# Reordering the join of a spectral block and the hand-over to its feed-forward: the order of early products, bank choices, load order and one LayerNorm tile on Trainium2

## The chip, the cores and the metric

The kernel runs on one core of one Trainium2 chip. The metric is the device time of one execution in microseconds (us); lower is better. Before the change the median of 4 runs is 252.41 us (251.09 to 253.37). The engines are named as the profile names them: PE (TensorE matmuls), PEld (its weight loads), DVE (VectorE), ACT (ScalarE), POOL (GpSimd) and SP (SyncE, which only issues transfers here). PSUM, the memory that matmuls write, has 8 banks.

## What is computed

```python
h = _layernorm(x) * (1 + ca) + sa
x = x + ga * irfft2(rfft2(h) * (w_r + 1j * w_i))
h = _layernorm(x) * (1 + cb) + sb
x = x + gb * ((silu(h @ w_gate) * (h @ w_up)) @ w_down)
```

`x` is 2048 x 640 in bf16. The six vectors sa, ca, ga, sb, cb, gb are the six parts of `silu(c) @ w_mod`, where `w_mod` is 640 x 3840. The spectral filter is 2048 x 321 complex; `w_gate` and `w_up` are 640 x 1728 and `w_down` is 1728 x 640.

## The kernel before, in words

**Stages.** The kernel has four stages. First, the forward transform along the 640 columns and its first step along the 2048 rows, tile by tile (16 tiles of 128 rows). Second, what this text calls the join: for the 81 frequency slots l (a slot holds four related columns), the last step of the forward row transform, the product with the filter, and the first steps back. Third, the rest of the inverse transform for the 16 row tiles t (line 1138), together with the residual and the statistics of the second LayerNorm. Fourth, the feed-forward over five chunks of 2, 4, 4, 4 and 2 tiles. The first of these chunks multiplies plainly (`gu_plain`, `down_plain`); the others use a scheme with fewer products (`gate_up_pairs`, `down_pair`).

**The join's groups.** The slots are in 21 groups (lines 509 to 511, `NG` = 21): groups 0 to 3 are l = 48 to 63, group 4 is l = 0 and 80, groups 5 to 16 are l = 1 to 47, groups 17 to 20 are l = 64 to 79. A group has four slots, except group 4 (two) and group 5 (three). For each group:

- `stage_a` (line 561): one matmul per slot (line 567) into the buffer `xps` of two banks, banks 2 and 3 for even groups and 4 and 5 for odd ones. Then DVE makes two products with the filter (`prod`, line 588): half 0 with the table `Wn`, half 1 with the table `Wv`, the filter stored in reversed order. So the matmuls of group g+2 write the banks that the products of group g read.
- `stage_b` (line 590): two matmuls per slot (line 595) add the parts, into bank g % 2; ACT copies the result to SBUF (line 598).
- `stage_c` (line 608) and `evac` (line 619): one more matmul per slot (line 616), and the copy to SBUF, mostly of two groups at once, out of banks 6 and 7. Afterwards POOL makes a turned copy (`rot`, line 644).

`wsum` (line 402) makes the third row of `Wn` or `Wv`, the sum of the other two, for a range of slots; products of these slots wait for it. `Wv` is read back from DRAM by two DMAs of line 426, the second one called `wflip_r` in the profile.

**Where the data of a group comes from.** `t2_pe` (line 533) transposes the slots of groups 0 to 4 on PE, ACT or DVE evacuates them. `t2_dma` (line 515) does so for the others by DMA transposes issued by SP: number 0 for l = 1 to 15, 1 for 16 to 31, 2 for 32 to 47, 3 for 64 to 79. For each of them POOL adds one column (`sa_add`, line 553, instruction at line 559) before `stage_a` may read it.

**Order.** Everything is issued in an order written out by hand, and every engine and the SP queue executes its own instructions in this order. Lines 673 to 685 begin the join: modulation matmuls `ga_mod` (line 649), the four `t2_pe`, `stage_a` of groups 0 and 1. The loop at line 686 then does, for each g: `sa_add(g + 4)`, `wsum` on POOL, `stage_a(g + 2)`, `stage_b(g)`, `stage_c` of earlier groups.

**Modulation of the second LayerNorm.** sb and cb come from 50 small matmuls (line 571) with `wm_r[:, :, 1:3]`, put inside `stage_a` of the last six groups, after its first matmul. `wm_r` is loaded by SP: part 0 early, parts 1 and 2 together at line 526 (1600 KB), part 3 at line 528.

**The hand-over.** In the loop over t at line 1138 the DVE instruction of line 1152 adds the residual and sums the row. For tiles 0 and 1, the first feed-forward chunk, `ln2_sq` (ACT, line 748) sums squares at t = 1 and 2, `ln2_var` (DVE, lines 752 to 754) and `ln2_pow` (POOL, line 758) come at t = 3, `ln2_xn` (DVE, line 762) at t = 4 and 5, and `ln2_tr` (line 776) at t = 5 issues the DMA transpose on SP. `ln2_mod` (POOL line 784 for four of the five blocks, ACT line 790 for the fifth) applies 1 + cb and sb. The first matmuls that need it are those of `gu13` (line 972), put at t = 15 just ahead of the last tile's matmuls. `load_gu` (line 731) loads a range of gate and up columns: 0 to 512 and 512 to 1024 ahead of the loop, 1024 to 1664 right after the DMA transpose.

**The first chunk.** The loop at line 1186 goes over 13 column blocks of 128, in the order 0, 6, 1, 7, 2, 8 and so on, with 10 matmuls a block (line 984).

Of the kernel before, what the change touches and what calls it, by code (L numbers as in the profile page):

```python
# [18 lines left out]
NT, P = 16, 128  # L19
NL = 81  # L20
NW = 256
NC5 = 5
# [133 lines left out]
def adaln_block_kernel(ctx, tc, A_x, A_w_r, A_w_i, B_x, B_w_gate, B_w_up, B_w_down, c, w_mod, out):  # L156
    nc = tc.nc
# [57 lines left out]
    Wn = rW.cut(0, [3, NT, NW])  # L215
    Wv = rW.cut(24576, [3, NT, NW])
# [108 lines left out]
    if True:  # L325
# [140 lines left out]
        for t in range(2, NT + 2):  # L466
# [4 lines left out]
            u = t + 2  # L471
# [39 lines left out]
    NG = len(groups)  # L511
    if True:
# [10 lines left out]
        t2_dma(0)  # L523
        t2_dma(1)
        t2_dma(2)
        nc.sync.dma_start(wm_r[:, :, 1:3, :], wm_m[:, :, 1:3, :])
        t2_dma(3)
        nc.sync.dma_start(wm_r[:, :, 3, :], wm_m[:, :, 3, :])
        nc.sync.dma_start(Htab[:], H_dram)
        nc.sync.dma_start(RI[:], RI_dram)  # L530
# [30 lines left out]
        def stage_a(g):  # L561
            ls = groups[g]
            n = len(ls)
            xps = banks(2 + 2 * (g % 2), 2, [4, 256])
            for i, l in enumerate(ls):
                B2, j = B2of[l][0:2]
                nc.tensor.matmul(xps[:, i, 0:192], lhsT=B2[:, j, :], rhs=KS2, start=True, stop=True)  # L567
                if i == 0:
                    for c5 in {NG - 6: (0, 1), NG - 5: (0, 1), NG - 4: (2, 3), NG - 3: (2,), NG - 2: (4,), NG - 1: (3, 4)}.get(g, ()):
                        for k in range(NC5):  # L570
                            nc.tensor.matmul(psum[:, 2 + 2 * (g % 2), 192 + c5:193 + c5],
                                             lhsT=wm_r[:, k, 1 + g % 2, 128 * c5:128 * c5 + 128],
                                             rhs=sc_col[:, k:k + 1], start=(k == 0), stop=(k == NC5 - 1))
            PP = rM.cut(1536 * (g % 4), [3, 2, NT, 2, n])
            prod(g, PP, xps, 0)
            prod(g, PP, xps, 1)
            return PP

# [10 lines left out]

        def stage_b(g, PP):  # L590
            n = len(groups[g])
            yps = banks(g % 2, 1, [4, 128])
            for ps in (1, 0):
                for i in range(n):
                    nc.tensor.matmul(yps[:, i, :], lhsT=_rev(PP, 64 * n * ps + i, [[n, 128]]), rhs=identb[:],  # L595
                                     start=(ps == 1 and i == 0), stop=(ps == 0 and i == n - 1))
# [11 lines left out]
        def stage_c(u):  # L608
            for g in units[u]:
                ls = groups[g]  # L610
                n, l0 = len(ls), ls[0]
                eps_ = banks({NG - 4: 4, NG - 3: 5, NG - 2: 1, NG - 1: 0}.get(g, 6 + (l0 // 4) % 2), 1, [4, 128])
                Y2 = Y2s.pop(g)
                for i, l in enumerate(ls):
                    kv = {0: 1, 80: 2}.get(l, 0)
                    nc.tensor.matmul(eps_[:, i + 4 - n if l0 else i, :], lhsT=Y2[:, i, :], rhs=Ktab[:, 128 * kv:128 * kv + 128],  # L616
                                     start=True, stop=True)

        def evac(u):
            g, l0 = units[u][0], groups[units[u][0]][0]  # L620
            if l0 == 0:
                edge = rY.cut(4096, [2, 128])
                nc.scalar.copy(edge[:], banks(6, 1, [4, 128])[:, 0:2, :])
                for i in range(2):
                    nc.gpsimd.tensor_copy(Em[:, :, :, 64 * i].rearrange("p v q -> p q v"),
                                          edge[:, i, :].rearrange("p (q v) -> p q v", v=2))
            elif g == NG - 2:
                nc.vector.tensor_copy(ep_views(l0, 4), banks(1, 1, [4, 128]).rearrange("p i q -> p q i"))
            elif g == NG - 1:
                nc.scalar.copy(ep_views(l0, 4), banks(0, 1, [4, 128]).rearrange("p i q -> p q i"))  # L630
            else:
                n = len(groups[g]) + 4
                (nc.vector.tensor_copy if g == NG - 6 else nc.scalar.copy)(
                    ep_views(l0, n), banks(4 if g == NG - 4 else 6, 2, [8, 128])[:, 8 - n:8, :].rearrange("p i q -> p q i"))
                if g < NG - 4:
                    rots.extend((l0, n, i) for i in range(1 if g == NG - 6 else 2))
# [36 lines left out]
        PPs, Y2s, rots = {}, {}, []  # L673
        ga_mod(320, 5, range(3))
        t2_pe(0)
        wsum(Wv, 48, 64, nc.vector)
        t2_pe(1)
        ga_mod(320, 5, range(3, NC5))
        PPs[0] = stage_a(0)
        t2_pe(2)  # L680
        t2_pe(3)
        wsum(Wn, 80, 81, nc.gpsimd)
        wsum(Wv, 80, 81, nc.gpsimd)
        PPs[1] = stage_a(1)
        ga_mod(0, 6, range(2))
        for g in range(NG + 1):
            sa_add(g + 4 if g > 0 else 0)
            for W, lo, hi in {0: ((Wv, 0, 16),), 1: ((Wv, 16, 32),), 3: ((Wv, 32, 48),), 11: ((Wn, 64, 80),), 13: ((Wv, 64, 80),)}.get(g, ()):
                wsum(W, lo, hi, nc.gpsimd)
            if g + 2 < NG:  # L690
                PPs[g + 2] = stage_a(g + 2)
            if g == 0:
                ga_mod(0, 6, range(2, NC5))
            if g == NG - 3:
                nc.vector.tensor_copy(modcols[:, 2, :], psum[:, 2, 192:197])
                nc.vector.tensor_copy(modcols[:, 3, :], psum[:, 4, 192:197])
                nc.vector.tensor_scalar_add(one_p_cb[:], modcols[:, 3, :], 1.0)
            if rots:
                l0, n, i = rots.pop(0)
                rot(l0, n, slice(0, 64), nc.gpsimd, (i,))  # L700
            if g < NG:
                Y2s[g] = stage_b(g, PPs.pop(g))
            for u, gs in enumerate(units):
                if gs[-1] + (1 if gs[0] >= NG - 2 else 3 if gs[0] == 4 else 2) == g:
                    stage_c(u)
                    evac(u)
            if g == NG - 1:
                rot(40, 8, slice(0, 64), nc.vector, (1,))
                nc.vector.tensor_tensor(RI[:, 1], RI[:, 1], ga_bc[:], ALU.mult)
# [18 lines left out]
    nc.sync.dma_start(Wp13[:, :, 0:64], B_w_gate[:, 1664:1728].rearrange("(c5 dp) f -> dp c5 f", dp=P))  # L728
    nc.sync.dma_start(Wp13[:, :, 64:128], B_w_up[:, 1664:1728].rearrange("(c5 dp) f -> dp c5 f", dp=P))

    def load_gu(lo, hi):
        nc.sync.dma_start(Wgu[:, 0, :, lo:hi], B_w_gate[:, lo:hi].rearrange("(c5 dp) f -> dp c5 f", dp=P))
        nc.sync.dma_start(Wgu[:, 1, :, lo:hi], B_w_up[:, lo:hi].rearrange("(c5 dp) f -> dp c5 f", dp=P))

    load_gu(0, 512)
    load_gu(512, 1024)

    x1 = rM.cut(0, [NT, D], F32)
    st2 = const.tile([P, NT, 2], F32, name="st2")
# [395 lines left out]
    if True:  # L1135
        VTs = {0: s1er(0), 1: s1er(1)}
        nc.vector.tensor_copy(gb_bc[:, 0:320], mod_bc(3, 0, 7))
        for t in range(NT):
            if t and t + 1 < NT:
                s1em(t + 1)  # L1140
                VTs[t + 1] = s1er(t + 1)
            VT = VTs.pop(t)
            if t == NT - 1:
                fin13 = gu13(0, at_of(0))
            ops = banks(6 * (t % 2), 2, [4, 256])[:, :, 0:160]
            for h in range(2):
                nc.tensor.matmul(ops[:, 2 * h:2 * h + 2], lhsT=VT[:, 4, :], rhs=RI[:, 1, 2 * h:2 * h + 2, :],
                                 start=True, stop=False)
                for rr in range(2):
                    nc.tensor.matmul(ops[:, 2 * h + rr], lhsT=VT[:, 2 * h + rr, :], rhs=RI[:, 0, 2 * h + rr, :],  # L1150
                                     start=False, stop=(rr == 1))
            nc.vector.scalar_tensor_tensor(x1[:, t, :].rearrange("p (m r) -> p m r", r=4), ops.rearrange("p r m -> p m r"), 1.0,
                                           x_sb[:, t, :].rearrange("p (m r) -> p m r", r=4), ALU.mult, ALU.add,
                                           accum_out=st2[:, t, 0:1])
            if t in (8, 11):
                gu_dma(GS[0][:], B_w_gate, t // 11 * 2, 2, t == 8)
            if 1 <= t <= 2:
                ln2_sq(t - 1)
            if t == 3:
                ln2_var(0, 2)  # L1160
                ln2_pow(0, 2)
            if 4 <= t <= 5:
                ln2_xn(0, t - 4)
            if t == 5:
                ln2_tr(0)
                load_gu(1024, 1664)
            if t in (5,7,9,11):
                ln2_sq(2 + (5,7,9,11).index(t))
            if t in (10, 13):
                ln2_mod(0, range(4) if t == 10 else range(4, 5))  # L1170
# [9 lines left out]
    for ci, (t0, n) in enumerate(chunks):  # L1180
# [3 lines left out]
            gate_up_pairs(ci, ATc, [lambda i=i: (ln2_xn_act(2, i), wd_tables(i, 1)) for i in range(4)] + [lambda: wd_tables(3, 0)] if ci == 1 else [])  # L1184
        else:
            for fc in range(NFC - 1):
                ff = fc if fc == 12 else fc // 2 + 6 * (fc % 2)
                half = gu_plain(ci, ATc, ff, (c3f, c22f)[fc % 2])
                half(0)
                half(1)  # L1190
# [91 lines left out]
```

## Time and profile before

| what | value |
|---|---|
| median of 4 runs | 252.41 us (251.09 to 253.37) |
| the profiled execution, its own time | 253.37 us |
| its span, first to last instruction | 251.6 us |
| granted TensorE clock in the span | 1.000 |
| PE busy | 243.5 us, 97% of the span |
| DVE, ACT, POOL busy | 210.5, 163.0, 74.9 us |
| moved by DMA | 34.43 MB, mean 137 GB/s |
| join and its end (first DVE product to first matmul of tile 0) | 40.4 to 66.4 us |
| inverse transform by tile | 66.4 to 84.7 us |
| first feed-forward chunk | 84.7 to 106.7 us |
| the other four chunks | 106.7 us to the end |

All times on a line of the profile count from the first instruction. A line of the timeline or of the chain gives start, length, engine, source line and how many instructions follow each other (x8); what stands in square brackets is how long the engine was idle before and what ended that. Matmuls are pipelined: the length of one overlaps the next, so the pace is read from the starts.

### The profile page before, as it was taken

The page shows a single profiled execution, that of the slowest core. Times are in us where ns is not written, and L with a number is a line of the kernel's source. Part 1 is how long each engine was busy: PE and PEld are TensorE (multiplying, and loading weights), DVE is VectorE, ACT ScalarE, POOL GpSimd, SP SyncE. Part 2 cuts the span into 40 slices and gives each one's busy share as a digit, 9 for nine tenths or more (in the row PEclk, how much of TensorE's full clock was granted, in tenths as well). Part 3 has the DMA queues.
Part 4 walks back from the last instruction along what each step waited for, and adds up shares of the span by engine and source line. Part 5 has one row for each costly group of instructions (what it writes and reads, how often), then busy time and mean ns, then how long its engine had stood idle before and what let it go on. Part 6 is the DMA issues. An engine that isn't in the chain of part 4 may idle for free.

```text
span 251.6 us, 6472 instructions
## 1 busy us (share of the span) xinstructions
PE 243.5 (97%) x2512; PEld 200.5 (80%) x2512; DVE 210.5 (84%) x524; ACT 163.0 (65%) x300; POOL 74.9 (30%) x122
## 2 busy tenths in 40 slices
PE   8999996999999999999999999999999999999994
PEld 3778875999789788788877778886768887779973
DVE  4798886998889998679997898879995978895895
ACT  3778664988788688678963577774267676235740
POOL 8487756695020905000001910000340000440000
PEclk9999999999999999999999999999999999999999
DMA  7999989999999999700005021001411000211001
GB/s 222 391 352 328 314 353 172 237 277 399 273 339 300 251 274 161 150 26 0 3 0 107 0 65 43 3 3 33 77 49 52 3 0 3 52 53 56 3 0 52
DMA packets 45760, 34.43 MB, mean 137 GB/s; under 512 B 21731, under 2 KB 42658, under 8 KB 45346
## 3 DMA queue, kind: packets, MB, share of 16 engines
q1 hardware_dynamic: 43936, 30.00, 42.8%
q0 software_dynamic: 1504, 3.95, 6.9%
q8 instruction: 19, 0.31, 0.5%
q10 hardware_dynamic: 290, 0.08, 0.1%
q14 instruction: 11, 0.09, 0.1%
HBM read 26.72 MB, written 4.72 MB: 125 GB/s over the span
## 4 chain that ended last, share of the span: by engine, by line
PE 72%; SPq 9%; DMA 9%; issue 4%; DVE 2%; POOL 1%; ACT 1%; DVEq 0%; POOLq 0%; ACTq 0%
PE psum L1014 32%; PE psum L897 19%; PE psum L984 9%; DMA rW<-wflip_r 4%; PE psum L595 3%; PE psum L877 3%; DMA rW<-rL 3%; SPq L277 2%; PE psum L567 2%; SPq L273 2%; DMA rM<-in_w_mod_dram 2%; SPq L275 2%; PE psum L972 2%; PE psum L616 2%; SPq L279 1%
## 5 line engine op out<-in xcount | busy, mean ns | idle before, releaser
L1014 PEld LDWEIGHTS <-rW 128*128 128x128 bf16 (+1 forms) x528 | 46.9, 98 | 5.7 <-issue 0.2
L1014 PE MATMUL psum<-rW 128*128 128x256 bf16 (+1 forms) x240 | 27.1, 259 | 0.0
L911 POOL TENSOR_TENSOR rM<-rM,rL 128x320 f32<-128x320 f32 x6 | 5.9, 977 | 68.3 <-ACT rL L910 68.3
L897 PEld LDWEIGHTS <-rE 128*128 128x128 f16 (+1 forms) x196 | 19.1, 97 | 7.7
L1014 PE MATMUL psum<-rY,rW 128*128 128x256 bf16 (+1 forms) x96 | 24.0, 259 | 0.0
L984 PE MATMUL psum<-rW 128*128 128x256 bf16 (+1 forms) x170 | 23.1, 291 | 0.0
L897 PE MATMUL psum<-rE 128*128 128x320 f16 (+1 forms) x147 | 22.3, 299 | 0.0
L588 DVE TENSOR_TENSOR rM<-psum,rW 128x384 bf16<-128x384 f32 (+2 forms) x42 | 20.0, 543 | 1.5 <-PE psum L567 0.9
L984 PEld LDWEIGHTS <-rW 128*128 128x128 bf16 x170 | 16.6, 98 | 3.8
L1014 PEld LDWEIGHTS <-rE 128*128 128x128 f16 x192 | 17.4, 98 | 2.4
L897 PEld LDWEIGHTS <-rX 128*128 128x128 bf16 (+1 forms) x151 | 14.5, 97 | 5.4
L758 POOL TENSOR_TENSOR rstd<-rstd,mhalf 128x4 f32<-128x4 f32 (+2 forms) x4 | 4.8, 1190 | 46.4 <-DVE rstd L754 46.4
L1050 DVE TENSOR_TENSOR rH<-psum,rW 128x512 bf16<-128x512 f32 x21 | 14.5, 690 | 4.7 <-PE psum L1014 2.8
L1046 ACT COPY rH<-psum 128x512 f32<-128x512 f32 x21 | 12.3, 586 | 8.7 <-PE psum L1014 7.0
L1053 ACT COPY rX<-psum 128x512 f32<-128x512 f32 x21 | 12.3, 587 | 6.9 <-PE psum L1014 6.9
L1040 ACT COPY rW<-psum 128x512 f32<-128x512 f32 x21 | 12.3, 586 | 6.8 <-PE psum L1014 6.6
L1068 DVE TENSOR_TENSOR rX<-rH,rL 128x512 bf16<-128x512 bf16 x21 | 8.9, 424 | 9.1 <-ACT rL L1066 9.0
L382 DVE SCALAR_TENSOR_TENSOR rE<-rE,mv,psum 128x648 bf16<-128x648 f32 (+1 forms) x17 | 14.2, 844 | 2.1 <-PE psum L318 1.5
L1054 DVE TENSOR_TENSOR rX<-psum,rX 128x512 f32<-128x512 f32 x21 | 14.4, 686 | 1.7 <-ACT rX L1053 1.6
L897 PE MATMUL psum<-rA,rX 128*128 128x320 bf16 (+1 forms) x98 | 15.6, 299 | 0.0
L1014 PE MATMUL psum<-rH,rW 128*128 128x256 f16 (+1 forms) x96 | 15.1, 259 | 0.1
L1014 PE MATMUL psum<-rE,rY 128*128 128x256 f16 (+1 forms) x96 | 15.1, 259 | 0.0
(198 smaller groups left out, 678.0 us busy)
## 6 DMA issues: line engine op xcount, KB each, us to landing
out_dram<-rA SPq DMA_DIRECT2D x31, 80.0 KB, 1.6
rM<-in_w_mod_dram SPq DMA_DIRECT2D x3, 800.0 KB, 9.2
rX<-in_A_x_dram SPq DMA_DIRECT2D x3, 640.0 KB, 7.4
rA<-in_B_w_down_dram SPq DMA_DIRECT2D x2, 960.0 KB, 11.1
rM<-in_w_mod_dram SPq DMA_DIRECT2D x1, 1600.0 KB, 8.2
rY<-in_B_w_gate_dram POOLq DMA_DIRECT2D x2, 768.0 KB, 7.2
rW<-in_B_w_gate_dram SPq DMA_DIRECT2D x2, 640.0 KB, 8.0
rW<-in_B_w_up_dram SPq DMA_DIRECT2D x2, 640.0 KB, 8.2
```

The lines of the kernel that those rows point to most:

```text
L382: nc.vector.scalar_tensor_tensor(Zv[:, h], Cv[:, h], mv[:, t, 0:1], zps[:, h], ALU.mult, ALU.subtract)
L588: nc.vector.tensor_tensor(PP[:, :, hl], xv[:, :, hl], in1, ALU.mult)
L595: nc.tensor.matmul(yps[:, i, :], lhsT=_rev(PP, 64 * n * ps + i, [[n, 128]]), rhs=identb[:], start=(ps == 1 and i == 0), stop=(ps == 0 and ...
L897: nc.tensor.matmul(o, lhsT=lhsT, rhs=rhs, start=start, stop=stop, skip_group_check=True)
L984: nc.tensor.matmul(gu[u], lhsT=Wgu[:, u, c5, ff * 128:(ff + 1) * 128], rhs=h2T[:, :, c5, :], start=(c5 == 0), stop=(c5 == NC5 - 1))
L1014: nc.tensor.matmul(o[:, f], lhsT=w, rhs=b, start=(start and f == 0 and i == 0), stop=(stop and f == F - 1 and i == len(ops) - 1), skip_gro ...
L1040: nc.scalar.copy(c0, X)
L1046: nc.scalar.copy(c2, X)
L1050: nc.vector.tensor_tensor(c11, Z, c0, ALU.add)
L1053: nc.scalar.copy(c3, X)
L1054: nc.vector.tensor_tensor(c22, Y, c3, ALU.add)
L1068: nc.vector.tensor_tensor(ato, v4(c11), v4(g21), ALU.mult)
```

## The change

It has two places.

In the join: the DMA transpose number 3 is issued ahead of the load of `wm_r[1:3]`; group 2 gets banks 6 and 7 for its first matmuls, and these are issued before the loop, right behind group 1's; the second half of the `ga_mod` matmuls is done in one piece in bank 0 instead of in two pieces in bank 6, and `stage_b` swaps its two banks accordingly, with the last two groups' banks swapped to match; DVE's sum of `Wv` for slots 48 to 63 is moved from ahead of group 0's products to between the two; POOL's sum of `Wv` for slot 80 moves into the loop, and the column add for DMA transpose 0 now stands ahead of the sum for slots 0 to 15 instead of behind it; the 50 small matmuls sit in the last four groups (10, 10, 15, 15) instead of the last six (10, 10, 10, 5, 5, 10).

In the hand-over: the variance, power, normalisation and DMA transpose of the first chunk come one tile sooner; of the loads of columns 512 to 1024 the gate part stays ahead of the DMA transpose and the up part goes behind it; the first chunk's blocks are taken in storage order.

```diff
         t2_dma(2)
+        t2_dma(3)
         nc.sync.dma_start(wm_r[:, :, 1:3, :], wm_m[:, :, 1:3, :])
-        t2_dma(3)
...
-            xps = banks(2 + 2 * (g % 2), 2, [4, 256])
+            xps = banks(6 if g == 2 else 2 + 2 * (g % 2), 2, [4, 256])
...
-                    for c5 in {NG - 6: (0, 1), NG - 5: (0, 1), NG - 4: (2, 3), NG - 3: (2,), NG - 2: (4,), NG - 1: (3, 4)}.get(g, ()):
+                    for c5 in {NG - 4: (0, 1), NG - 3: (0, 1), NG - 2: (2, 3, 4), NG - 1: (2, 3, 4)}.get(g, ()):
...
             prod(g, PP, xps, 0)
+            if g == 0:
+                wsum(Wv, 48, 64, nc.vector)
             prod(g, PP, xps, 1)
...
-            yps = banks(g % 2, 1, [4, 128])
+            yps = banks((g + 1) % 2, 1, [4, 128])
...
         t2_pe(0)
-        wsum(Wv, 48, 64, nc.vector)
         t2_pe(1)
         ga_mod(320, 5, range(3, NC5))
         PPs[0] = stage_a(0)
         t2_pe(2)
         t2_pe(3)
         wsum(Wn, 80, 81, nc.gpsimd)
-        wsum(Wv, 80, 81, nc.gpsimd)
         PPs[1] = stage_a(1)
-        ga_mod(0, 6, range(2))
+        ga_mod(0, 0)
+        PPs[2] = stage_a(2)
         for g in range(NG + 1):
-            sa_add(g + 4 if g > 0 else 0)
-            for W, lo, hi in {0: ((Wv, 0, 16),), 1: ((Wv, 16, 32),), 3: ((Wv, 32, 48),), 11: ((Wn, 64, 80),), 13: ((Wv, 64, 80),)}.get(g, ()):
+            if g > 1:
+                sa_add(g + 4)
+            for W, lo, hi in {0: ((Wv, 80, 81), (Wv, 0, 16)), 1: ((Wv, 16, 32),), 3: ((Wv, 32, 48),), 11: ((Wn, 64, 80),), 13: ((Wv, 64, 80),)}.get(g, ()):
                 wsum(W, lo, hi, nc.gpsimd)
-            if g + 2 < NG:
+                if g == 0 and hi == 81:
+                    sa_add(5)
+            if 0 < g < NG - 2:
                 PPs[g + 2] = stage_a(g + 2)
-            if g == 0:
-                ga_mod(0, 6, range(2, NC5))
...
-    def load_gu(lo, hi):
-        nc.sync.dma_start(Wgu[:, 0, :, lo:hi], B_w_gate[:, lo:hi].rearrange("(c5 dp) f -> dp c5 f", dp=P))
-        nc.sync.dma_start(Wgu[:, 1, :, lo:hi], B_w_up[:, lo:hi].rearrange("(c5 dp) f -> dp c5 f", dp=P))
+    def load_gu(lo, hi, us=(0, 1)):
+        for u in us:
+            nc.sync.dma_start(Wgu[:, u, :, lo:hi], (B_w_gate, B_w_up)[u][:, lo:hi].rearrange("(c5 dp) f -> dp c5 f", dp=P))
 
     load_gu(0, 512)
-    load_gu(512, 1024)
+    load_gu(512, 1024, (0,))
...
-            if t == 3:
+            if t == 2:
                 ln2_var(0, 2)
                 ln2_pow(0, 2)
-            if 4 <= t <= 5:
-                ln2_xn(0, t - 4)
-            if t == 5:
+            if 3 <= t <= 4:
+                ln2_xn(0, t - 3)
+            if t == 4:
                 ln2_tr(0)
+                load_gu(512, 1024, (1,))
                 load_gu(1024, 1664)
...
-                ff = fc if fc == 12 else fc // 2 + 6 * (fc % 2)
+                ff = fc
```

The diff leaves out the swap of banks 0 and 1 for the last two groups in `stage_c` and `evac`.

More of the change, by code (lines that the diff above doesn't have):

```diff
@@ L611, in stage_c @@
                 n, l0 = len(ls), ls[0]
-                eps_ = banks({NG - 4: 4, NG - 3: 5, NG - 2: 1, NG - 1: 0}.get(g, 6 + (l0 // 4) % 2), 1, [4, 128])
+                eps_ = banks({NG - 4: 4, NG - 3: 5, NG - 2: 0, NG - 1: 1}.get(g, 6 + (l0 // 4) % 2), 1, [4, 128])
                 Y2 = Y2s.pop(g)
@@ L627, in evac @@
             elif g == NG - 2:
-                nc.vector.tensor_copy(ep_views(l0, 4), banks(1, 1, [4, 128]).rearrange("p i q -> p q i"))
+                nc.vector.tensor_copy(ep_views(l0, 4), banks(0, 1, [4, 128]).rearrange("p i q -> p q i"))
             elif g == NG - 1:
-                nc.scalar.copy(ep_views(l0, 4), banks(0, 1, [4, 128]).rearrange("p i q -> p q i"))
+                nc.scalar.copy(ep_views(l0, 4), banks(1, 1, [4, 128]).rearrange("p i q -> p q i"))
             else:
```

## The prediction, made before the changed kernel was run

> **What bounds the kernel.** I read the page first: PE is busy 97% of the span, so only time in which PE stands still in front of work can be won. Past the start-up, the list of waits names two places where PE waits 0.5 us or more for another engine, and the change touches both. Then I read each engine's timeline around them. First the start of the join on DVE and PE:
>
> ```profile
> 40.06 0.43 DVE L407 TENSOR_TENSOR rW<-rW 128x512 bf16<-128x512 bf16 x1 [2.65 <-DMA rW<-wflip_r]
> 40.40 3.80 DVE L588 TENSOR_TENSOR rM<-psum,rW 128x384 bf16<-128x384 f32 x8
> ...
> 38.20 0.49 PE L567 MATMUL psum<-Ktab,rM 128*128 128x192 bf16 x4
> 38.53 0.43 PE L649 MATMUL psum<-rM,sc_rep 128*128 128x320 bf16 x2
> 41.47 0.49 PE L567 MATMUL psum<-Ktab,rM 128*128 128x192 bf16 x4 [2.50 <-DVE rM L588]
> 41.80 0.57 PE L649 MATMUL psum<-rM,sc_rep 128*128 128x320 bf16 x3
> 42.20 0.61 PE L595 MATMUL psum<-identb,rM 128*128 128x128 bf16 x8
> ```
>
> DVE stands still for 2.65 us until `wflip_r` has landed, makes the sum, and only then begins products without a pause. PE stops for 2.50 us because group 2's matmuls write the banks of group 0's products. Second, the end of the tile loop on PE and POOL:
>
> ```profile
> 82.93 0.55 PE L972 MATMUL psum<-rW,Wp 128*128 128x256 bf16 x3
> 83.99 0.38 PE L972 MATMUL psum<-rW,Wp 128*128 128x256 bf16 x2 [0.51 <-POOL rW L784]
> ...
> 81.53 2.41 POOL L784 TENSOR_SCALAR rW<-rW,one_p_cb,modcols 128x256 bf16<-128x256 bf16 x4 [8.03 <-DMA rW<-rL]
> ```
>
> POOL waits for the DMA transpose of the first chunk, and PE for POOL. From 84.75 to 106.7 PE has no gap, and the chain runs on PE nearly to the end, so what is won ahead of 84.75 stays won. Third, the SP queue, which the change also reorders:
>
> ```profile
> 36.79 8.10 SPq L519 DMA_TRANSPOSE rL<-rA  x3
> 44.93 1.19 SPq L526 DMA_DIRECT2D rM<-in_w_mod_dram  x1
> 46.24 6.66 SPq L519 DMA_TRANSPOSE rM<-rA  x1
> 52.95 0.58 SPq L528 DMA_DIRECT2D rM<-in_w_mod_dram  x1
> ```
>
> **What the Trainium skill says.** "PSUM — Partial Sum Buffer", section "Engine vs sequencer instructions": the VectorE, ScalarE and GpSimd queues are strictly first in, first out. The trace agrees: group 0's half-0 product needs only `Wn` and matmuls that ended at 37.8 (start 37.27, four in 0.54), yet it starts at 40.40, behind the sum. "DMA: Bandwidth & Descriptors", section "Queues, rings and completion order": each DMA engine consumes one queue's descriptors in ring order. The trace agrees: `wm_r[1:3]` is issued at 44.93, but by the packet records its flow begins at 47 to 48, after transpose 2 (256-byte packets until 46.8); transpose 3 flows from 51.9, as `wm_r` runs out, and lands at 54.93. The same page, "Latency and other measured facts", gives a DMA transpose with a non-contiguous middle dimension 261 GB/s; here transpose 3, 2048 packets of 256 B, takes 2.4 us, 220 GB/s.
>
> **The join, part by part.**
>
> *DVE's sum between the two halves.* Eight full products take 3.80 us, the last one 0.55, so their pitch is (3.80 - 0.55) / 7 = 0.464. After the change product (0,0) runs at 37.8 in DVE's idle time; behind the landing come the sum (40.06) and then (0,1) at 40.40. Every later product takes the place of its predecessor: 0.46 sooner. Half 1 of group 0 is the first that needs the sum, so nothing new waits.
>
> *Group 2 in banks 6 and 7, `ga_mod` in one piece.* Four L567 (0.33 by their starts, 41.47 to 41.80) and three L649 (0.40) move from behind the wait into PE's idle time. `ga_mod` now needs bank 0, which ACT clears of `t2_pe(2)` at 38.65, so five L649 run at 38.7 to 39.4 and group 2 at 39.4 to 39.7: all before 40. `stage_b(0)` starts when (0,1) ends, 40.95, instead of 42.20. Is that 1.25 kept? No. Before, group 5's matmuls start at 44.26, the moment product (3,1) frees banks 4 and 5 (43.66 + 0.55 = 44.20). They still need (3,1), now 0.46 sooner: 43.79. In between PE has to do `stage_b(0)` 0.45, `stage_a(3)` 0.33 (from 41.93, behind (1,1)), `stage_b(1)` 0.45, `stage_a(4)` 0.17, `stage_b(2)` 0.45, which ends about 43.3, so it waits for DVE. PE's lead shrinks to DVE's 0.46, and from there PE is full: a pair of groups takes 2.0 us at 50.3 to 54.3, which is 8 x 0.082 + 16 x 0.056 + 8 x 0.056. So the early move of group 2 is worth nothing beyond DVE's shift; without it PE's extra 0.73 would eat into its slack there.
>
> *POOL's order.* `sa_add(5)` waits for DMA transpose 0 (landing 42.39, add 42.46). The sum for slots 0 to 15, 1.15 us, was done before it (until 41.74); now it follows, 42.64 to 43.80. First to read it is product (4,1), due at about 44.05: cover 0.25 us. If transpose 0 lands x later, DVE loses x - 0.25. The next two sums move from 42.64-44.92 to 43.8-46.05, into POOL's idle time up to 46.82; their readers, groups 9 and 13, come after 48.
>
> *Fifty small matmuls.* Ten take 0.25 (54.41 to 54.66). Their sum stays; the last `stage_a` holds 15 ahead of its other three matmuls but the earlier ones give the time back. Cost 0.
>
> *DMA transpose 3 ahead of `wm_r[1:3]`.* It now follows transpose 2 directly and lands at about 50 instead of 54.93; its first reader, group 17, comes at 56.8, so no gain. But `wm_r` comes later. Its first reader is the first L571 of group 17, before at 56.91; after: 56.91 - 0.46 - 0.50 (the twenty that leave groups 15 and 16) = 55.95. Estimate of its landing: transpose 3's issue took 6.66 us because it sat behind `wm_r`; it ended when `wm_r`'s packets had run out. Behind transpose 2 alone (out at 46.8), with the 1.4 us by which issue ends trailed the previous transfer before (43.09 to 44.89, previous packets out at 43.5), it ends at 48.2. Then 1.3 us to first packet (as L528), 1600 KB at the 370 GB/s of the packet records 4.4, and 0.9 to the landing: 54.8, 1.1 us in time. Upper bound, an issue as long as before: 51.6 + 6.6 = 58.2, 2.3 us too late. Lower bound: 0. I take 0. Behind it on SP stand part 3, `Htab`, `RI` and the weights, with the same bytes ahead of them; `Htab` landed at 61.3 with its reader at 64.3.
>
> Join: -0.46.
>
> **The hand-over.** PE's five L972 have a pitch of 0.11; the fourth should follow the first by 0.33 (83.26) and starts at 83.99: 0.73 lost in all (the view says 0.51, counting from the modelled end). The DMA transpose was issued at 74.64, after the second L762. After the change, in the old time frame: the variance follows tile 2's residual (70.2) and waits for ACT's second square sum (70.45), ends at 70.7; POOL's power 0.70 to 71.45; tile 3's residual to 71.43; first L762 to 72.0; tile 4's residual 0.82; second L762 to 73.4. So issue at 73.45, 1.2 us sooner. At 6.7 us as before it lands 80.1, POOL's four blocks (0.19 + 2.41) end at 82.75, and the fourth matmul wants its block at 83.26: wait gone, margin 0.5. Uncertain is only the flight: 3.4 to 8.8 us among the five. Ahead of it in the ring now stands 640 KB less (up 512 to 1024), which favours the short side; POOL's own load, in flight with it, can stretch it. The burst on DVE (tiles 2 to 5) moves a tile ahead with the same instructions; tile 4's residual ends at 72.85 and PE needs its banks at 73.31, so PE doesn't stop. If that cover is gone, it is at most the 0.48 of the variance.
>
> The up part of 512 to 1024 is issued at about 76 and, with 8 to 9.6 us to land as its like, is there by 86. In storage order it is needed by block 4, at 84 + 4 x 1.09 = 88; in the old order block 6 would have come second, at 85. That is what the order pays for: without it a stall of about 1 us. Columns from 1024 are needed at block 8, 92.7, and landed at 87.1. Cost 0.
>
> Hand-over: -0.73, between 0 and -0.73.
>
> **Sum.** Span 251.59 - 0.46 - 0.73 = 250.4; that execution 253.37 - 1.19 = 252.2; it lies 0.96 above the median, so the median goes from 252.41 to 251.2. That is 0.5%, less than the about 1% that a measurement of this kernel can tell from no change.
>
> **Rivals.** *A, the forecast*, 251.2, chance 0.62, own range 250.6 to 251.9.
> *B, `wm_r` becomes the wait*, chance 0.14: the L571 of group 17 hold PE. For it speaks the 6.66 us issue; against it, that the cause of that issue is now behind it. It costs from a landing at 55.95, cancels all from 57.1, and at the bound 58.2 gives 251.2 + 2.3 = 253.5, slower than before. Its middle is 252.2.
> *C, the transpose of the first chunk is not earlier relative to PE*, because POOL's load takes its engines: only the join counts, 252.41 - 0.46 = 251.95, chance 0.10.
> *D, the join's 0.46 is lost* at POOL's sum behind `sa_add(5)` or at ACT's evacuations: 251.7, chance 0.07.
> *E, more than the sum*, because idle spots further on (0.33 at 49.61 to 49.94, 0.31 at 63.4) close too: 250.5, chance 0.07.
>
> **From these to the numbers.** A, C, D and E lie between 250.3 and 252.1; B reaches 253.5, and runs of one kernel scatter by 1 us around their median. 250.3 to 252.8 leaves out the late half of B and about a tenth for scatter. Faster by over 1% (below 249.9) needs E and scatter: 0.05. Slower by over 1% (above 254.9) needs B beyond its bound: 0.03. Within 1%: 0.92.
>
> **What would show it.** Right: one L588 before 40 us and the sum behind it; L595 first at about 41.0; group 5's L567 at 43.8; L571 without a wait on `wm_r`; the issue of L776 at about 73, no wait of L972 on L784; L984 first at about 83.5. Wrong: a DMA wait at L571 or at group 4's second product; L972 still waiting; PE gaps between 85 and 106, which would be late weights.

## The result, and the profile after

The changed kernel takes 251.82 us, the median of 43 runs (250.55 to 255.23); the kernel before, run beside it, takes 252.6 us (64 runs, 251.09 to 255.75). The ratio is 0.9968, with a 95% interval of 0.9953 to 0.9982, so about 0.8 us are won, between 0.45 and 1.2. The forecast was 251.2, with a range of 250.3 to 252.8.

The profiled execution of the changed kernel took 251.35 us, its span is 249.57. That is 2.02 less than the 251.59 of before, more than the runs show. I cut both spans at the landing of `wflip_r`, the first thing that both joins wait for. Its DMA is issued at 29.35 in the trace of before, and what the change moves begins past 37. Here t0 is the first matmul of tile 0 (L1147 before, L1149 after).

| stretch | before | after | difference |
|---|---|---|---|
| start to the landing of `wflip_r` | 39.97 | 38.47 | -1.50 |
| landing to t0 (the join) | 26.44 | 26.70 | +0.26 |
| t0 to the first matmul of the feed-forward | 18.35 | 17.62 | -0.73 |
| from there to its first down matmul | 14.19 | 14.19 | 0.00 |
| from there to the end | 152.65 | 152.59 | -0.06 |

The first row is not the change's: over the fourteen kernels profiled here `wflip_r` landed anywhere from 38.28 to 40.79. The hand-over gave what was predicted, and the join, which should have given 0.46, lost 0.26. The timeline of the kernel after shows why; in it L590 is the product that was L588, L597 was L595, L651 was L649, and L974 was L972. DVE and PE at the start and the end of the join:

```profile
37.89 0.56 DVE L590 TENSOR_TENSOR rM<-psum,rW 128x384 bf16<-128x384 f32 x1 [0.43 <-PE psum L567]
38.56 0.43 DVE L407 TENSOR_TENSOR rW<-rW 128x512 bf16<-128x512 bf16 x1
39.02 4.21 DVE L590 TENSOR_TENSOR rM<-psum,rW 128x384 bf16<-128x384 f32 x9
...
39.43 0.49 PE L567 MATMUL psum<-Ktab,rM 128*128 128x192 bf16 x4
39.76 0.61 PE L597 MATMUL psum<-identb,rM 128*128 128x128 bf16 x8
40.56 0.49 PE L567 MATMUL psum<-Ktab,rM 128*128 128x192 bf16 x4 [0.20 <-DVE rM L590]
...
42.42 0.41 PE L567 MATMUL psum<-Ktab,rL 128*128 128x192 bf16 x3 [0.29 <-DVE rM L590]
...
54.49 0.25 PE L567 MATMUL psum<-Ktab,rM 128*128 128x192 bf16 x1
55.16 0.40 PE L571 MATMUL psum<-sc_col,rM 128*128 128x1 bf16 x10 [0.42 <-DMA rM<-in_w_mod_dram]
```

The product (0,0) runs while DVE waits, and the 2.50 us of PE's idle time are gone from the front. Group 5's matmuls start 3.95 after the landing instead of 4.29: a gain of 0.34. But the last line is new. The small matmuls L571 now wait for `wm_r[1:3]`. They should start 0.08 after the L567 ahead of them, the pitch of an L567; they start 0.67 after it. So 0.59 is lost, more than the join had won. SP's queue and the hand-over, on POOL and PE:

```profile
36.83 6.87 SPq L519 DMA_TRANSPOSE rL<-rA  x3
43.81 4.11 SPq L519 DMA_TRANSPOSE rM<-rA  x1
47.96 0.59 SPq L527 DMA_DIRECT2D rM<-in_w_mod_dram  x1
...
72.25 1.58 SPq L778 DMA_TRANSPOSE rW<-rL  x1
73.89 0.59 SPq L735 DMA_DIRECT2D rW<-in_B_w_up_dram  x1
...
78.44 2.41 POOL L786 TENSOR_SCALAR rW<-rW,one_p_cb,modcols 128x256 bf16<-128x256 bf16 x4 [7.33 <-DMA rW<-rL]
...
81.70 0.71 PE L974 MATMUL psum<-rW,Wp 128*128 128x256 bf16 x5
82.25 0.30 PE L1149 MATMUL psum<-rH,rL 128*128 128x320 bf16 x1
```

The load of `wm_r[1:3]` (L527) is issued at 47.96, 3.0 us later than before, and lands at 55.12. The five L974 follow each other without a pause: POOL has its transposed tile 3 us ahead of them.

### The profile page after: what moved, and what is told of

It is laid out like the page before. It is cut to its first block, busy times and chain, and to the rows that moved or that the text cites. A ratio compares the mean times of both kernels' runs of the same rounds, so it can differ in the third digit from the quotient of the medians.

```text
span 249.6 us, 6473 instructions
## 1 busy us (share of the span) xinstructions
PE 243.6 (98%) x2512; PEld 200.6 (80%) x2512; DVE 209.8 (84%) x524; ACT 162.9 (65%) x300; POOL 74.6 (30%) x122
## 3 DMA queue, kind: packets, MB, share of 16 engines
q0 software_dynamic: 1504, 3.95, 6.7%
## 4 chain that ended last, share of the span: by engine, by line
PE 78%; SPq 9%; DMA 8%; ACT 1%; DVE 1%; issue 1%; DVEq 0%; ACTq 0%
PE psum L1016 33%; PE psum L899 19%; PE psum L986 9%; DMA rM<-in_w_mod_dram 5%; DMA rW<-wflip_r 4%; PE psum L879 3%; PE psum L664 3%; SPq L273 2%; SPq L277 2%; PE psum L1149 2%; SPq L275 2%; PE psum L597 2%; PE psum L1152 2%; PE psum L974 2%; SPq L279 2%; PE psum L567 1%
## 5 line engine op out<-in xcount | busy, mean ns | idle before, releaser
L590 DVE TENSOR_TENSOR rM<-psum,rW 128x384 bf16<-128x384 f32 (+2 forms) x42 | 20.1, 543 | 2.5 <-PE psum L567 1.2
```

The source lines that it names most:

```text
L590: nc.vector.tensor_tensor(PP[:, :, hl], xv[:, :, hl], in1, ALU.mult)
```

## The experiments

Times are medians beside runs of the kernel before on the same chip. A ratio is the one on record with its 95% interval; it is not the quotient of the two medians. Shorter times such as 0.33 are differences between starts in a trace. Line numbers shift by a few lines from kernel to kernel, and a comment such as `# e3` in a diff only names the kernel.

### Each half of the change alone

`e1_hand_only` is the kernel before with only the hand-over's edits; `e2_join_only` is the kernel after with the hand-over's edits undone.

> The kernel before with the hand-over edits alone (LayerNorm of the first chunk a tile sooner, up part of 512 to 1024 behind the DMA transpose, blocks in storage order). My theory: the fourth L972 follows the first by 0.33 us instead of 1.06, so 0.73 us sooner than before from the start of the feed-forward on; time 0.2 to 0.4% below before. Rival, that the gain of the whole change comes from the join: no change here (within 0.1%).

> The changed kernel with the hand-over edits undone, so the join edits alone. Theory 'taken back': products run 0.34 to 0.46 us sooner behind the landing of the filter, but group 17's first small matmul then waits for the late modulation load (0.59 us lost in the profiled run of the change), so from the landing of wflip_r to the first matmul of tile 0 it takes 26.4 to 26.7 us as before (26.43) and the time is within 0.15% of before. Rival 'no wait as a rule': the wait came only with that run's early landing (38.47), the span from landing to tile 0 is 26.0 to 26.1, and the time is 0.15 to 0.2% below before.

e1: t0 to the feed-forward 17.63, so the 0.73 is the hand-over's and needs nothing of the join. The time is 251.76 against 252.36, ratio 0.9995 (0.9968 to 1.0023): the interval is too wide for 0.3% and just holds it. Its join was not free of loss either. Transpose 3 landed at 55.41, which is 16.8 after the filter (15.0 in the trace of before), so POOL's column add was late and group 17 started 0.35 late:

```profile
55.49 0.27 POOL L559 TENSOR_TENSOR rM<-rM,SA 128x16 bf16<-128x16 bf16 x1 [1.91 <-DMA rM<-rA]
```

So the kernel before has a transfer of its own that is sometimes late. Why it was late here is open.

e2: group 5 comes 3.95 after the landing, as in after, but the wait for `wm_r[1:3]` (landing 56.37) is longer and takes all of the join's gain and more: t0 comes 27.66 after the landing. Time 252.46, ratio 1.0004 (0.9984 to 1.0023). By the times alone, then, neither half is shown to win; what each half brings is read from the traces.

```profile
54.78 0.25 PE L567 MATMUL psum<-Ktab,rM 128*128 128x192 bf16 x1
56.42 0.40 PE L571 MATMUL psum<-sc_col,rM 128*128 128x1 bf16 x10 [1.39 <-DMA rM<-in_w_mod_dram]
```

From 54.78 to 56.42 are 1.64 instead of 0.08: 1.55 lost. This is rival B of the prediction, at the place that it named.

### Is it the order of the transfers?

`e3_wm_split` is after with part 2, which the first small matmuls read, loaded ahead of part 1; `e4_wm_first` is after with transpose 3 behind the load again, as before the change.

```diff
-        nc.sync.dma_start(wm_r[:, :, 1:3, :], wm_m[:, :, 1:3, :])      # e3
+        nc.sync.dma_start(wm_r[:, :, 2, :], wm_m[:, :, 2, :])
+        nc.sync.dma_start(wm_r[:, :, 1, :], wm_m[:, :, 1, :])
...
-        t2_dma(3)                                                       # e4
         nc.sync.dma_start(wm_r[:, :, 1:3, :], wm_m[:, :, 1:3, :])
+        t2_dma(3)
```

> The changed kernel with the load of parts 1 and 2 of the modulation cut in two, the part that group 17 reads first (part 2, 800 KB) issued first. Theory 'taken back': part 2 lands about 2 us sooner (53 us), the wait of the small matmuls is gone, landing to tile 0 takes 26.0 to 26.1 us, and the time is 0.1 to 0.25% below the changed kernel, 0.4 to 0.55% below before. Rival 'no wait as a rule': within 0.05% of the changed kernel, 0.3% below before.

> The changed kernel with the modulation load ahead of DMA transpose 3 again, as before. Both theories: the modulation lands by about 53 and no small matmul waits; DMA transpose 3 lands at 54 to 55 and its column add on POOL ends 0.3 later, so group 17's first matmul (due at 54.5 to 55.5) waits 0 to 0.8 us. If the swap of the two transfers is needed, the time is 0.1 to 0.3% above the changed kernel; if it costs as much as it saves, the same within 0.1%.

In e3 part 2 lands at 53.09 and the wait is gone; L571 (here L572) follows its L567 at the full pace, and t0 comes 26.09 after the landing, 0.35 sooner than before the change:

```profile
54.90 0.25 PE L568 MATMUL psum<-Ktab,rM 128*128 128x192 bf16 x1
54.99 0.39 PE L572 MATMUL psum<-sc_col,rM 128*128 128x1 bf16 x10
```

e4's trace says the same, t0 at 26.09. So the join's gain is 0.34 to 0.35 where no late transfer eats it and product (0,0) is done when the filter lands. In e7 below it was not done: the filter landed at 38.28, and the sum, behind the product on DVE, had to wait.

```profile
38.13 0.56 DVE L590 TENSOR_TENSOR rM<-psum,rW 128x384 bf16<-128x384 f32 x1 [0.43 <-PE psum L567]
38.60 0.41 DVE L407 TENSOR_TENSOR rW<-rW 128x512 bf16<-128x512 bf16 x1
```

The sum began 0.32 after the landing instead of 0.09, and of the gain 0.13 was left.

The times agree only in part. e3 takes 251.52, ratio 0.9957 (0.9937 to 0.9977), about the 1.07 us that 0.34 and 0.73 make; e4 takes 252.43, ratio 1.0005 (0.9981 to 1.0029), which excludes that gain. In e4's profiled execution transpose 3 landed 14.7 after the filter and its reader, group 17, came at 16.0, so nothing waited. A landing at 16.8 after the filter, as in e1, would have bound. That is argued; how often it happens in e4, and so why e4's times show no gain, was not measured.

Eight traces have the load order of after. They show what moves this transfer; `wm_r[1:3]` is counted from the filter's landing, and the wait is that of the first L571:

| kernel | filter lands | issue of transpose 0 ends | `wm_r[1:3]` lands | that is, after the filter | wait |
|---|---|---|---|---|---|
| e7 | 38.28 | 38.79 | 54.45 | 16.17 | 0 |
| after | 38.47 | 38.53 | 55.12 | 16.65 | 0.59 |
| e9 | 38.50 | 38.85 | 54.97 | 16.47 | 0.33 |
| e5 | 38.62 | 38.75 | 55.02 | 16.40 | 0.34 |
| e6 | 38.67 | 39.33 | 54.67 | 16.00 | 0 |
| e2 | 38.76 | 39.22 | 56.37 | 17.61 | 1.55 |
| e8 | 39.35 | 39.99 | 55.59 | 16.24 | 0.18 |
| e11 | 40.79 | 40.79 | 57.02 | 16.23 | 0 |

In e6, with the sum ahead, and in e11, with the clock stretch told at the end, L571 itself is due later. The load moves with the filter. In all fourteen traces the issue of transpose 0 on SP starts at 36.70 to 37.16 and ends 0.0 to 0.7 after the filter has landed, and what stands behind it on SP is pushed back with it. SP of e7 and of e11, where the filter landed 2.5 later:

```profile
37.07 6.90 SPq L519 DMA_TRANSPOSE rL<-rA  x3
47.46 0.59 SPq L527 DMA_DIRECT2D rM<-in_w_mod_dram  x1
```

```profile
36.74 8.80 SPq L519 DMA_TRANSPOSE rL<-rA  x3
49.67 0.59 SPq L527 DMA_DIRECT2D rM<-in_w_mod_dram  x1
```

### What the join's gain is made of

`e5_group2_late` takes group 2 out of its extra banks and back into the loop. `e6_sum_ahead` puts DVE's sum ahead of both products of group 0 again.

```diff
-            xps = banks(6 if g == 2 else 2 + 2 * (g % 2), 2, [4, 256])  # e5
+            xps = banks(2 + 2 * (g % 2), 2, [4, 256])
...
-        PPs[2] = stage_a(2)
...
-            if 0 < g < NG - 2:
+            if g < NG - 2:
...
-            if g == 0:                                                  # e6
-                wsum(Wv, 48, 64, nc.vector)
...
         t2_pe(0)
+        wsum(Wv, 48, 64, nc.vector)
         t2_pe(1)
```

> The changed kernel with group 2's first matmuls back in banks 2 and 3 and back in the loop, behind group 0's products. My prediction called the early move worth nothing: the time from the landing of wflip_r to group 5's first matmul stays 3.95 us (within 0.05), because that matmul waits for a product. Rival, that PE's lead counts: 0.3 to 0.7 us more.

> The changed kernel with DVE's sum of Wv for slots 48 to 63 ahead of both products of group 0 again. From the landing of wflip_r to group 5's first matmul it takes 3.95 us in the changed kernel and 4.29 before. If the order of the sum is the whole of the join's gain, this run gives 4.29; if the early group 2 has a part in it, 4.1. The first product should start 0.34 us after the sum, as before, instead of 0.46 as in the changed kernel, where the product reads the sum just made.

e5 has group 5 at 3.95, the same as after: the early group 2 and its banks are worth nothing. e6 has it at 4.29, the same as before: the order of DVE's sum is the whole gain, and the rest of the join's edits, `ga_mod` in one piece among them, bring nothing without it. One line of DVE for e6:

```profile
39.10 4.19 DVE L588 TENSOR_TENSOR rM<-psum,rW 128x384 bf16<-128x384 f32 x9
```

The sum starts at 38.76 there, and the next product, (0,0), which does not read it, 0.34 later. In after the next product is (0,1), which reads what the sum has just written, and it starts 0.46 later (38.56 to 39.02). The difference of 0.12 is what the join's gain falls short by: 0.46 - 0.12 = 0.34. The step from the sum to the next product is 0.34 in all three traces with a half-0 product there (before, e1, e6) and 0.44 to 0.46 in the eleven with a half-1 product. That the reading of the fresh sum makes it longer is argued: the two products also differ in their half, and no run separates the two. One run each: e5 251.33 and e6 251.3, beside 251.83 for the kernel before.

### The hand-over: the sooner tile, the cut load, the block order

`e8_up_ahead` keeps the sooner tile but loads gate and up together ahead of the loop. `e9_tile_late` keeps the cut load but issues the transpose a tile later, as before. `e7_old_blocks` takes the first chunk's blocks in the old order.

```diff
-    load_gu(512, 1024, (0,))                                            # e8
+    load_gu(512, 1024)
...
-                load_gu(512, 1024, (1,))
...
-            if t == 2:                                                  # e9
+            if t == 3:
                 ln2_var(0, 2)
                 ln2_pow(0, 2)
-            if 3 <= t <= 4:
-                ln2_xn(0, t - 3)
-            if t == 4:
+            if 4 <= t <= 5:
+                ln2_xn(0, t - 4)
+            if t == 5:
...
-                ff = fc                                                 # e7
+                ff = fc if fc == 12 else fc // 2 + 6 * (fc % 2)
```

> The changed kernel with the first chunk's column blocks in the old order (0, 6, 1, 7 and so on), so that block 6 comes second and reads the up columns that are now loaded behind the DMA transpose. My prediction said about 1 us of PE stall there, from a landing at up to 86 us. The trace of the changed kernel shows the up part landed at 80.3 and the feed-forward begun at 82.8: then no stall, and the 130 matmuls of the chunk take 14.2 us as before.

> The changed kernel with both parts of columns 512 to 1024 loaded ahead of the DMA transpose again. Theory 'a tile is enough': the DMA transpose still lands 6 to 7 us after its issue at about 72.3, by 79.3, and the fourth L974 follows the first by 0.33 us: the cut of the load was not needed. Rival 'the ring': with 640 KB more ahead of it it takes 8 us or more, lands past 80, and part of the wait (up to 0.5 us) is back.

> The changed kernel with the LayerNorm of the first chunk a tile later again (as before), but the up part of columns 512 to 1024 still behind the DMA transpose. With both parts ahead and a tile sooner the transpose took 8.0 us and the wait was back in full. If the cut of the load alone is what counts: issue about 73.4 (1.2 us later than in the changed kernel), 6.0 us to land, POOL's four blocks end 2.6 us later at about 82.0 to 82.3, and the fourth L974 follows the first by 0.33 to 0.6 us. If both are needed: 0.8 us or more.

The two halves of the hand-over make four cases, and each was run (e2 is a second look at the first):

| tile | up part | kernel | issue after t0 | landing after t0 | fourth matmul after the first |
|---|---|---|---|---|---|
| as before | ahead | before, e2 | 8.24, 8.23 | 14.94, 15.14 | 1.05, 1.36 |
| sooner | ahead | e8 | 7.08 | 15.11 | 1.32 |
| as before | behind | e9 | 8.23 | 12.75 | 0.33 |
| sooner | behind | after | 7.08 | 13.08 | 0.33 |

The transpose's landing follows the row's second column, not its first. With the up part's 640 KB ahead of it in the ring, an issue 1.15 us sooner brings the landing not a tenth of a microsecond nearer: the flight grows from 6.7 and 6.9 to 8.0. With the 640 KB behind it, the late tile lands in time too, after a flight of 4.5. The late tile with the 640 KB behind has one trace, but the nine other traces with both edits (e1, e3 to e7, e10 to e12) agree with the row of after: landings of 12.2 to 13.9, and 0.33 each. Of the two theories in e8's expectation the rival, the ring, held. SP, POOL and PE of e8, where the old wait is back:

```profile
72.72 3.38 SPq L778 DMA_TRANSPOSE rW<-rL  x1
...
80.94 2.49 POOL L786 TENSOR_SCALAR rW<-rW,one_p_cb,modcols 128x256 bf16<-128x256 bf16 x4 [9.36 <-DMA rW<-rL]
...
82.95 0.27 PE L974 MATMUL psum<-rW,Wp 128*128 128x256 bf16 x1 [0.40 <-POOL rW L786]
83.48 0.38 PE L974 MATMUL psum<-rW,Wp 128*128 128x256 bf16 x2 [0.27 <-POOL rW L786]
```

And of e9, where the issue is 0.53 later, counted from each trace's start, and the landing (77.77 against 80.75) 3 us sooner:

```profile
73.25 2.03 SPq L778 DMA_TRANSPOSE rW<-rL  x1
...
77.96 2.39 POOL L786 TENSOR_SCALAR rW<-rW,one_p_cb,modcols 128x256 bf16<-128x256 bf16 x4 [5.86 <-DMA rW<-rL]
...
81.54 0.71 PE L974 MATMUL psum<-rW,Wp 128*128 128x256 bf16 x5
```

The order of the blocks is worth nothing in e7's trace: from the first feed-forward matmul to the first down matmul it takes 14.19, as every kernel here. The up part landed at 79.55 there, 2.7 us ahead of the feed-forward's first matmul at 82.2. One run each: e7 251.53 and e8 253.57 beside 251.83 for the kernel before, e9 251.16 beside 252.08.

### Towards a better version

In five of the twelve traces up to here (e2, e3, e7, e8, e10) the stretch from the first down matmul to the end is 153.3 instead of 152.6. The lines of e5, which has 152.65, and of e7, which has 153.35, at the same place of the second chunk; DVE's add first, then POOL's that starts beside it:

```profile
137.54 0.61 DVE L855 TENSOR_TENSOR rE<-rX 128x896 f16<-128x896 bf16 x1
...
137.56 1.31 POOL L922 TENSOR_TENSOR rM<-rM,rL 128x320 f32<-128x320 f32 x1
```

```profile
137.08 1.36 DVE L856 TENSOR_TENSOR rE<-rX 128x896 f16<-128x896 bf16 x1
...
137.10 0.85 POOL L923 TENSOR_TENSOR rM<-rM,rL 128x320 f32<-128x320 f32 x1
```

The two adds start within 0.02 of each other; one takes its usual time and the other 0.5 to 0.75 more. Where DVE is the one that waits, the end is 0.7 later. The Trainium skill, "SBUF — State Buffer", section "Who interferes with whom", says that a VectorE instruction with two SBUF inputs contends with a GpSimd instruction that reads SBUF, and that the order of issue decides which of the two blocks. That one of the two is slowed agrees with it. What decides which one is not shown: in all twelve traces DVE's add starts 0.02 ahead of POOL's, whichever of them is the slow one.

`e10_two_ahead` puts a second product, (1,0), ahead of the sum, as DVE has time for it before the filter lands, puts POOL's sum for slots 0 to 15 back ahead of the column add, and takes e3's load order. `e11_nb_late` is after with `ln2_nb(10, 6)`, a small DVE instruction that waits for POOL's power, moved behind DVE's sums of the second chunk, so that the two adds no longer meet. `e12_best` is both.

```diff
+        held = []                                                       # e10
...
             if g == 0:
+                held.append((PP, xps))
+                return PP
+            if g == 1:
                 wsum(Wv, 48, 64, nc.vector)
+                prod(0, *held.pop(), 1)
             prod(g, PP, xps, 1)
...
-                if g == 0 and hi == 81:
+                if g == 0 and hi == 16:
                     sa_add(5)
...
-                ln2_nb(10, 6)                                           # e11
...
+                    if ci == 1 and i == 4:
+                        ln2_nb(10, 6)
```

> Not in the change: the changed kernel with the modulation load cut in two (as in the third experiment), and half 0 of group 1 also ahead of DVE's sum, so that two products use the wait for the filter; POOL's sum for slots 0 to 15 goes ahead of the column add again, since its reader comes sooner. If DVE's products after the landing set the pace: landing to group 5's first matmul 3.95 - 0.46 = 3.5 us, and to tile 0 26.1 - 0.46 = 25.6 if PE can follow. If PE is the limit by now: 3.7 or more and 25.9 or more.

> Not in the change: in four of ten traces so far DVE's first sum of A parts in the second half of chunk 1 takes 1.36 us instead of 0.61, beside a POOL add, and the rest of the run is 0.7 us later (152.6 or 153.3 us from the first down matmul to the end). Here the small DVE instruction that waits for POOL's power goes behind these sums, so that they run 2 us sooner, ahead of POOL's adds. If the collision on that stretch is the cause: 152.6 us or less in this stretch, the median 0.1 to 0.2% below the changed kernel's and fewer runs at the upper end. Rival: the sums then collide with POOL's power instead, and nothing is won.

> Everything that looked better, on top of the change: modulation load cut in two, two products ahead of the sum, the small DVE instruction of chunk 1 behind the sums. Adding the parts: 0.3 us (no modulation wait), 0.3 to 0.46 (one more product in the idle time), 0 to 0.35 (collision) below the changed kernel, so about 0.55 to 0.75% below before. If PE or a later wait takes it back: within 0.1% of the changed kernel, 0.3% below before.

e10: 251.81 in one run. In its trace the second early product was not finished when the filter landed, so the sum began 0.64 after the landing and group 5 came at 4.02, no sooner than in after. In e12 the sum began 0.25 after it and group 5 came at 3.63: another 0.32 won. What that brings thus depends on when the filter lands. More than that was lost again in e12, 0.56, at the second piece of the split load, which landed at 56.29, later than group 18's small matmuls wanted it:

```profile
55.70 0.25 PE L570 MATMUL psum<-Ktab,rM 128*128 128x192 bf16 x1
56.34 0.40 PE L574 MATMUL psum<-sc_col,rM 128*128 128x1 bf16 x10 [0.39 <-DMA rM<-in_w_mod_dram]
```

So t0 came 26.34 after the landing in e12, later than the 26.09 of e3.

e11 and e12: the add takes 0.62 and the last stretch 152.54 and 152.53. Two traces do not show that the late outcome is gone, only that it did not occur. e11 takes 251.64, ratio 0.9971 (0.9949 to 0.9993), so the further 0.1 to 0.2% that was expected of it is not shown; e12 251.12, ratio 0.9953 (0.9935 to 0.997), the lowest median and the narrowest spread of all kernels (20 runs, 250.97 to 251.72). It was expected 0.55 to 0.75% below before and is 0.47% below. Its interval overlaps that of after, so it is not shown to be better than it.

## Why the prediction was right, step by step

- **The total** (251.2, range 250.3 to 252.8, within 1%) holds: 251.82, a gain of 0.8 where 1.19 was summed. The interval is 0.3% wide and excludes a ratio of 1, although the prediction took about 1% for the least that a measurement of this kernel can tell. The hand-over gave 0.73 in the traces. What the join gave differs from execution to execution: in the seven traces with the join of after (e5, with group 2 late, counted in) t0 comes 26.3 to 27.7 after the filter's landing, in the two with the join of before 26.4 and 26.8. So the 0.8 is close to the hand-over alone, and the join's share of it is not shown.
- **"Every later product takes the place of its predecessor: 0.46 sooner"** is 0.12 too much: the step left out that the product behind the sum is now one that reads the sum and starts 0.46 after it instead of 0.34, and the trace of before had no such pair to take a pitch from. e6 against after measures it. It also took for granted that (0,0) is done when the filter lands; in e7 it was not, and 0.13 was left.
- **"The early move of group 2 is worth nothing beyond DVE's shift"** holds: 3.95 in e5 and 3.95 in after. PE had DVE to wait for at group 5 in both.
- **POOL's order** cost nothing: the column add came at 41.36 and the sums right behind it, and DVE's nine products behind the sum ran without a pause. The 50 small matmuls cost nothing beyond their wait: without it t0 comes 0.35 sooner (e3, e4), which is the join's whole gain.
- **"54.8, 1.1 us in time ... I take 0"** is the step that failed. Counted from the filter's landing at 39.97, its due time was right: 55.95 is 16.0 after it, and 16.1 was measured (e3, e4). Its landing was too soon: 54.8 is 14.8 after it, and in the eight traces of the table above the load landed 16.0 to 17.6 after the filter. In after the 16.65 are 1.8 more than forecast: 0.3 had been lost when the issue of transpose 2 ended (5.2 after the filter instead of 4.9), 0.9 went to the issue of transpose 3 (it ended 4.2 after that of transpose 2 instead of 3.3), and 0.6 to the way from there to the landing (7.2 instead of 6.6). That 54.8 lies near the 55.12 of the trace is chance; the filter was 1.5 sooner there. Rival B had the mechanism and the place and was given 0.14. It showed in five of the eight traces. It costs part of the gain, and in e2 all of the join's, but does not make the kernel slower.
- **The hand-over, -0.73**, is exact in size, and that is luck, because its reason is wrong. The issue is 1.15 sooner (1.2 forecast), the five matmuls have no wait. But "at 6.7 us as before" treats the flight as the transfer's own. It is mostly the bytes ahead of it: e8 has the sooner issue and keeps the wait, e9 has the late issue and loses it. The cut of the load, which the step named only as what "favours the short side", is the whole effect. The page of the Trainium skill quoted in the prediction, "DMA: Bandwidth & Descriptors", section "Queues, rings and completion order", says that a DMA engine consumes one queue's descriptors in ring order; the four cases agree with it, and the step should have been worked out from it.
- **"Without it a stall of about 1 us"** for the old block order is wrong: e7 stalls by 0.00. The up part was taken to need 8 to 9.6 us from about 76 on; in e7 it had landed at 79.55, and in after at 80.29, 6.4 us after its issue at 73.89.
- **Rivals C, D and E.** C's outcome did not come: the landing is 1.9 us sooner after t0. Whether POOL's load slows the transpose at all was not tested. D's places, POOL's sum and ACT's evacuations, have no wait. E's further gain past the join did not appear; the stretches behind the feed-forward's start are equal to 0.06.

## What to carry to other kernels

Count the due time of a transfer and its landing both from the event that they follow, not from the start of the trace. Here both followed the filter's landing, which moved by 2.5 us from one execution to another; the load's place behind it moved by 1.6, so a slack has to be read from several traces and not from one. When a transfer is late, look first at the bytes ahead of it in its queue and only then at when it is issued; taking 640 KB from in front did what an issue 1.15 us sooner did not. A gain early in a kernel should be checked against the next transfer that is due, since at 0.3 us a step it is easily eaten by one.

## What the runs showed of the hardware that I had not expected

A product on DVE that reads the result of the sum just ahead (128x512 in bf16) starts 0.44 to 0.46 us after the sum's start in eleven traces; one that does not read it 0.34 in three. The two also differ in their half, as said above.

The issue of a DMA transpose on SP took 1.7 to 4.1 us (transpose 0, fourteen traces) and ended 0.0 to 0.7 us after an earlier transfer of the same queue, the filter, had landed.

Two adds on DVE and POOL that start within 0.02 us of each other went one way in seven traces and the other way in five, with DVE's start ahead by 0.02 in all twelve, and that moved the end by 0.7 us.

In e11's trace the filter landed at 40.79, and PE, busy until 39.83, paused for 2.13 us until 41.96. At 42.37 the granted clock was halved, to 0.50, until 45.78; the columns are busy time of PE, PEld, DVE, ACT and POOL, then the clock, the DMA share and GB/s:

```profile
42.00:43.00 1.00, 0.80 (x10) 0.63 (x11) 1.00 (x3) 0.28 (x1) 0.00 (x0) 0.69 1.21 271
43.00:44.00 1.00, 1.00 (x9) 0.96 (x8) 1.00 (x3) 0.31 (x1) 0.71 (x2) 0.50 1.27 289
46.00:47.00 1.00, 1.00 (x20) 1.00 (x19) 0.82 (x2) 0.74 (x2) 0.85 (x1) 1.00 1.17 217
```

Nine of the join's matmuls fell into one microsecond at 0.50, twenty at 1.00 (not the same mix of them); group 5 came at 4.71 after the landing instead of 3.95. A stretch of 3.4 us at half rate makes a mean clock of 0.993 over 252 us. Means of 0.990 to 0.993 are on record for eight of the hundred executions of the kernel before that stand beside e1 to e4 and e9 to e12, all of 253.7 us or more, and for two of after's, 254.01 and 255.23. The Trainium skill, "TensorE: Matmul & The Clock Gate", section "What's actually happening", states half rate after at least one idle window of about 3.4 us, in windows that run freely. The length of the halved stretch, about 3.4 us, agrees. The condition does not: a pause of 2.13 us was enough here, while the 2.50 us pause of the kernel before left the clock at 1.00. Why the one and not the other stays open.
